# Products in two tiles, softmax four ahead and moved x loads: one change to a tuned convolution and two-layer product

## The chip, the cores and the metric

The kernel runs on one core of a Trainium2 chip. The time is the device time of one execution in microseconds (us). "Span" is the profiled execution from its first to its last instruction, about 1.8 us shorter than the time of the same run.

## The reference

```python
w = softmax(weight_gen, axis=-1)               # batch 8, 4096 tokens, 8 heads, 7 taps
x_pad = concat([zeros(6 tokens), x])           # 192 channels, 24 for each head
conv[s, h, g] = sum over k of w[s, h, k] * x_pad[s + k, h, g]
h = conv.reshape(32768, 192) @ w_in            # 192 x 2048
out = (h - tanh(h)) @ w_out                    # 2048 x 192, float32
```

## The kernel before

The 32768 tokens are cut into 32 superblocks of 1024. Each token's seven taps are multiplied by GpSimd. Some of the seven products are then added by DMAs that accumulate in SBUF ("first sum", "second sum"); TensorE transposes what is left and adds it up in PSUM ("the transposes"). Pass n of the loop runs the first product (line L354) of superblock n in 16 steps f, weaves in the second product (L389) of earlier blocks, and near its end, at steps 13 and 14, transposes superblock n+1 (L311). GpSimd meanwhile makes the products of n+2.

```python
xpool  = tile_pool(bufs=2)      # x
wgpool = tile_pool(bufs=2)      # weight_gen, its exponential e_t, the softmax wsm
ppool  = tile_pool(bufs=2)      # pr: one tile of all seven taps
TWO_SUMS = [n for n in range(13, NTOT) if n % 3]        # 13 superblocks
# ... products(n), from superblock 5 on:
mul(nc.gpsimd, 0, 2)
second_sum(n - 1)                       # taps 0,1 += taps 2,6   (n-1 in TWO_SUMS)
mul(nc.gpsimd, 2, 6)
dma_sum(pr, 0, 3, 3, 6)                 # first sum: taps 0-2 += taps 3-5
mul(nc.gpsimd, 6, K)
prods_of[n] = parts(0, 1) if n in TWO_SUMS else parts(6, 0, 1, 2)
# ... pass n:
f == 1:   softmax_exp(n + 3); load_wg(n + 4); products(n + 2)
f == 7:   load_x(n + 3, last_sub[0])    # from SyncE, behind the subtraction of step 7
f == 13:  transposes(n + 1, (0, 1))
f == 14:  transposes(n + 1, (2,))
```

The output of a superblock is stored once per pass, also from SyncE.

The softmax here doesn't subtract the row's maximum and nothing guards it: scores larger than these inputs give would overflow.

Of the kernel before, what the change touches and what calls it, by code (L numbers as in the profile page):

```python
# [16 lines left out]
def kernel(  # L17
# [18 lines left out]
    J = 8  # L36
# [6 lines left out]
    NC = D // R  # L43
    PLAIN = (0, 1)
    PART = tuple(range(2,5))
    TWO_SUMS = tuple([n for n in range(13,NTOT) if n%3])
    SUM_FIRST = tuple(range(5,32))
    SCALE_TWICE = True
# [4 lines left out]
    xpool = ctx.enter_context(tc.tile_pool(name="xpool", bufs=2))  # L53
    wgpool = ctx.enter_context(tc.tile_pool(name="wgpool", bufs=2))
    ppool = ctx.enter_context(tc.tile_pool(name="ppool", bufs=2))
    cpool = ctx.enter_context(tc.tile_pool(name="cpool", bufs=2))
# [28 lines left out]
    last_conv = {}  # L85
    first_halo = {}

    def order(inst, other, reason):
# [17 lines left out]
    def load_x(n, behind=None):  # L106
# [23 lines left out]
        if n == 0:  # L130
            rows(0, P, HALO, HALO + J)
            rows(16, P, 0, HALO)
            rows(1, 16, 0, HALO)
            no_halo()
        else:
            dma = rows(0, P)
            if behind is not None:
                order(dma, behind, "order of the loads")
            if s == 0:

                no_halo()
        x_of[n] = x_t

    def softmax_exp(n):
        wg_t = wg_of.pop(n)
        e_t = wgpool.tile([P, J, H, K], FP32, name="e_t")
        last_exp[0] = nc.scalar.activation(  # L147
            out=e_t[:].rearrange("p j h k -> p (j h k)"),
            in_=wg_t[:].rearrange("p j h k -> p (j h k)"),
            func=ACT.Exp,  # L150
        )
        e_of[n] = e_t

    def softmax_tile():
        return wgpool.tile([P, J, H, K], FP32, name="wsm")

# [14 lines left out]

    def softmax_norm(n, bank):

        wsm = softmax_tile()
        zr_v = bank[:, 512 - J * H : 512]
        nc.vector.reciprocal(zr_v, zsum_of[n][:])  # L176

        def finish():
            scale(nc.vector, wsm[:], e_of[n], zr_v)
            wsm_of[n] = (wsm, None, None, None)  # L180

        return finish

# [28 lines left out]

    def dma_sum(pr, k0, k1, src0, src1, step=1):
        nc.gpsimd.dma_start(  # L214
            out=pr[:, k0:k1].rearrange("p k j d -> p k (j d)"),
            in_=pr[:, src0:src1:step].rearrange("p k j d -> p k (j d)"),
            accum_op=mybir.AluOpType.add,
            max_dma_last_dim=2 * J * D,
        )

    def products(n, taps=None, sums=None, hooks={}):
# [5 lines left out]

        pr = ppool.tile([P, K, J, D], BF16, name="pr")
        x_v = x_t[:]
        step = x_v.ap[0]  # L230

        def mul(eng, k0, k1, j0=0, j1=J):

            w = wsm_v if eng is nc.vector else wsm[:]
            nj = j1 - j0
            return eng.tensor_mul(  # L236
                pr[:, k0:k1, j0:j1, :].rearrange("p k j (h g) -> p k (j h) g", h=H),
                bass.AP(
                    tensor=x_v.tensor,
                    offset=x_v.offset + (k0 + j0) * D,  # L240
                    ap=[step, [D, k1 - k0], [G, nj * H], [1, G]],
                ),
                w[:, j0:j1]
                .rearrange("p j h (k o) -> p k (j h) o", o=1)[:, k0:k1]
                .to_broadcast([P, k1 - k0, nj * H, G]),
            )

        def parts(*ks):
            return [[pr[:, k] for k in ks]] * NC

# [9 lines left out]

        if n in PLAIN:
            mul(nc.gpsimd, 0, 3)
            mul(nc.gpsimd, 3, 5)
            mul(nc.gpsimd, 5, K)
            prods_of[n] = parts(*range(K))
        elif n in PART:
            mul(nc.gpsimd, 0, 2)
            mul(nc.gpsimd, 2, 4)
            dma_sum(pr, 0, 2, 2, 4)
            mul(nc.gpsimd, 4, K)  # L270
            prods_of[n] = parts(4, 5, 6, 0, 1)
        else:
            mul(nc.gpsimd, 0, 2)
            second_sum(n - 1)
            mul(nc.gpsimd, 2, 6)
            if n in SUM_FIRST:
                dma_sum(pr, 0, 3, 3, 6)
            mul(nc.gpsimd, 6, K)
            if n not in SUM_FIRST:
                dma_sum(pr, 0, 3, 3, 6)  # L280
            if n in TWO_SUMS:
                to_sum[n] = pr
                prods_of[n] = parts(0, 1)
            else:
                prods_of[n] = parts(6, 0, 1, 2)
            if n == NTOT - 1:
                second_sum(n)

    def second_sum(n):

        if n in to_sum:
            dma_sum(to_sum.pop(n), 0, 2, 2, K, 4)

# [55 lines left out]
    def gemm1(n, f):  # L349
# [18 lines left out]
        last_sub[0] = nc.vector.tensor_sub(gt[:], ph_f, th[:])  # L368
        g_of.setdefault(n, []).append(gt)

    LAST = (NTOT - 1) * J
# [140 lines left out]
    for c in range(NC):  # L512
# [4 lines left out]
        1,  # L517
        taps=[(V, 0, 1, 0, J), (V, 1, 2, 0, J), (G_, 2, 5, 0, J), (G_, 5, 7, 0, J)],
        sums=range(K),
        hooks={2: load_w_out},  # L520
    )
# [3 lines left out]
    softmax_norm_ramp(2, obank[0])  # L525
    products(2)

# [30 lines left out]
    FIRST = dict(pairs=(4, 12, 0, 16, 1, 15, 0, 16, 0, 16, 0, 13, 3, 0, 16, 16), t1=(15, 2), t2=(11, 10), scale=15, sums=(1, 2, 3, 4, 8, 10))  # L558
    X_AT = 7

    def transposes(n, chunks):
# [4 lines left out]
        return pcs[0]  # L566

    for n in range(1, NTOT):
        more = n < NTOT - 1
        finish = None  # L570
        plan = FIRST if n == 1 else STEADY
        for f in range(NFT):
            gemm1(n, f)
            if n == 1:
# [8 lines left out]
                if f == 5:  # L583
                    wsm_of[3] = (softmax_tile(), None, e_of[3], zr_of[3])
                    products(3)
            elif f == 1:
                if n + 3 < NTOT:
                    softmax_exp(n + 3)
                if n + 4 < NTOT:
                    load_wg(n + 4)  # L590
                if n < NTOT - 2:
                    products(n + 2)
            if n > 1 and n + 3 < NTOT:
                for h, at in enumerate(plan["sums"]):
                    if f == at:
                        softmax_sum(n + 3, h * JH, (h + 1) * JH)
            if f == X_AT and n + 3 < NTOT:
                load_x(n + 3, last_sub[0])
            done = 0
            for chunks, at in sorted((((0, 1), plan["t2"]), ((2,), plan["t1"])), key=lambda c: c[1]):  # L600
                if more and at[0] == f:
                    out_pairs(at[1] - done)
                    done = at[1]
                    pc = transposes(n + 1, chunks)
                    if chunks == (2,) and n + 3 < NTOT:
                        finish = softmax_norm(n + 3, pc[:, 0])
            if finish is not None and f >= plan["scale"]:
                finish()
                finish = None
            out_pairs(plan["pairs"][f] - done)  # L610
# [36 lines left out]
```

## Time and profile before

| | before |
|---|---|
| median of the first 3 runs | 752.21 us (752.07 to 753.29) |
| span of the profiled run | 751.4 us, mean granted clock 0.994 |

Pass lengths and waits are read off in the prediction. Two more pieces of the same profile matter later. The first is part of the page's list of DMA issues (size of one, median time from issue to landing) with the row of the queue that brings instructions (packets, MB, share of the 16 engines' time):

```profile
q8 instruction: 109, 1.79, 0.9%
...
x_t<-in_x_dram SPq DMA_DIRECT2D x31, 1344.0 KB, 6.0
pr<-pr POOLq DMA_DIRECT2D x27, 1152.0 KB, 9.9
out_dram<-out_sb SPq DMA_DIRECT2D x31, 768.0 KB, 3.4
```

The second is who TensorE waited for between 60 and 747 us, beside the one wait for the second sum:

```profile
PE ph L354 <- issue: 0.6, 1, 0.6
PE obank L389 <- issue: 0.5, 2, 0.3
```

"issue" stands for time in which the engine waited for nothing that the profile knows.

### The profile page before, as it was taken

To read this page: it belongs to the slowest core of one execution; us is meant where nothing else is said; L and a number is where in the kernel's file an instruction comes from. 1 tells how busy PE (TensorE), PEld (TensorE's weight loads), DVE (VectorE), ACT (ScalarE), POOL (GpSimd) and SP (SyncE) were. 2 spreads that over 40 slices of the span, in tenths; PEclk is the share of its full clock that TensorE was granted. 3 is DMA by queue.
4 is the path that set the end of the run, shared out by engine and by line. 5 is a ranking of instruction groups with operands and counts; after the bars stand their busy time and mean duration, and the time that the engine had idled before them with its cause. 6 is when DMAs were issued, how large, how long until landed. Compare 5 with 4: busy or idle time off the path is not lost.

```text
span 751.4 us, 30497 instructions
## 1 busy us (share of the span) xinstructions
PE 725.4 (97%) x13928; PEld 567.6 (76%) x13928; DVE 664.6 (88%) x655; ACT 638.8 (85%) x872; POOL 668.9 (89%) x150
## 2 busy tenths in 40 slices
PE   3899999999999999999999999999999699999998
PEld 2477887787887777777777777777787577777777
DVE  7999889998889998999999999999989589998983
ACT  4888888888888888898989899898989588988883
POOL 7999999999999999999999999999999988999000
PEclk9999999999999999999999999999999899999999
DMA  8944526665655567785796777579668658673412
GB/s 234 242 111 107 171 109 173 187 181 126 191 149 170 169 170 160 202 196 163 196 229 151 180 203 185 169 196 215 173 157 192 180 139 189 183 177 85 113 44 86
DMA packets 32511, 124.99 MB, mean 166 GB/s; under 512 B 4495, under 2 KB 9343, under 8 KB 28414
## 3 DMA queue, kind: packets, MB, share of 16 engines
q0 software_dynamic: 17664, 46.01, 35.7%
q1 hardware_dynamic: 14718, 77.03, 27.6%
q8 instruction: 109, 1.79, 0.9%
q14 instruction: 20, 0.16, 0.1%
HBM read 54.52 MB, written 25.17 MB: 106 GB/s over the span
## 4 chain that ended last, share of the span: by engine, by line
PE 49%; DMA 4%; POOL 4%; issue 0%; ACT 0%; DVE 0%; POOLq 0%; DVEq 0%
PE obank L389 23%; PE ph L354 22%; DMA pr<-pr 4%; POOL pr L236 4%; PE pc L311 2%; PE po L432 1%; ACT th L367 0%; DVE wsm L207 0%; POOL pr L214 0%; ACT convT L337 0%; DVE pc L176 0%; DVE out_sb L446 0%; ACT ot L445 0%; DVE gt L368 0%; POOLq L214 0%
## 5 line engine op out<-in xcount | busy, mean ns | idle before, releaser
L368 DVE TENSOR_TENSOR gt<-ph,th 128x1024 bf16<-128x1024 f32 x512 | 603.1, 1218 | 66.8 <-ACT th L367 66.2
L236 POOL TENSOR_TENSOR pr<-x_t,wsm 128x3072 bf16<-128x3072 f32 (+3 forms) x95 | 629.7, 6816 | 8.1 <-PE obank L389 3.4
L367 ACT ACTIVATE th<-ph 128x1024 f32<-128x1024 f32 x512 | 506.8, 1026 | 71.1 <-PE ph L354 66.9
L354 PE MATMUL ph<-convT,w_in 64*128 64x512 bf16 x3072 | 407.3, 380 | 5.0 <-DVE gt L368 3.2
L389 PEld LDWEIGHTS <-gt 64*128 64x128 bf16 x7936 | 353.0, 94 | 73.0 <-issue 11.7
L389 PE MATMUL obank<-w_out,gt 64*128 64x192 bf16 x7936 | 399.5, 243 | 0.6 <-issue 0.5
L354 PEld LDWEIGHTS <-w_in 64*128 64x128 bf16 x3072 | 171.5, 95 | 82.7 <-issue 12.2
L408 ACT ACTIVATE out_sb<-obank 128x192 f32<-128x192 f32 x248 | 82.4, 332 | 12.9 <-PE obank L389 10.4
L214 POOL DMA_DIRECT2D pr<-pr x43 | 54.9, 1276 | 20.4 <-DMA pr<-pr 11.0
L311 PEld LDWEIGHTS <-pr 64*128 64x128 bf16 x2664 | 51.9, 102 | 24.1 <-POOL pr L236 10.2
L311 PE MATMUL pc<-ident,pr 64*128 64x64 bf16 x2496 | 50.7, 194 | 16.6 <-POOL pr L236 10.1
L337 ACT ACTIVATE convT<-pc 128x1024 bf16<-128x1024 f32 (+1 forms) x62 | 50.5, 816 | 7.3 <-PE pc L311 6.7
L161 DVE TENSOR_REDUCE zsum<-e_t 128x32 f32<-128x224 f32 (+1 forms) x61 | 23.6, 387 | 3.0 <-ACT e_t L147 3.0
L147 ACT ACTIVATE e_t<-wg_t 128x448 f32<-128x448 f32 x32 | 18.2, 569 | 7.3 <-DMA wg_t<-in_weight_gen_dram 7.3
L207 DVE TENSOR_TENSOR wsm<-e_t,pc 128x448 f32<-128x448 f32 x28 | 17.4, 621 | 3.3 <-POOL pr L236 0.5
L176 DVE RECIPROCAL pc<-zsum 128x64 f32<-128x64 f32 x28 | 15.4, 551 | 0.1
L432 PE MATMUL po<-w_out,gt 64*128 64x192 bf16 x256 | 11.2, 243 | 0.0
L236 DVE TENSOR_TENSOR pr<-x_t,obank 128x1536 bf16<-128x1536 f32 (+4 forms) x8 | 10.3, 1349 | 0.6 <-ACT wsm L199 0.6
L432 PEld LDWEIGHTS <-gt 64*128 64x128 bf16 x256 | 10.8, 93 | 0.0
L446 DVE TENSOR_TENSOR out_sb<-po,ot 128x192 f32<-128x192 f32 x8 | 2.9, 358 | 9.0 <-ACT ot L445 9.0
L445 ACT ACTIVATE ot<-po 128x192 f32<-128x192 f32 x8 | 2.6, 331 | 7.3 <-PE po L432 7.3
L467 POOL DMA_DIRECT2D w_in<-in_moe_w_in_dram x4 | 2.5, 628 | 3.0 <-ACT e_t L147 3.0
(19 smaller groups left out, 18.3 us busy)
## 6 DMA issues: line engine op xcount, KB each, us to landing
x_t<-in_x_dram SPq DMA_DIRECT2D x31, 1344.0 KB, 6.0
pr<-pr POOLq DMA_DIRECT2D x27, 1152.0 KB, 9.9
out_dram<-out_sb SPq DMA_DIRECT2D x31, 768.0 KB, 3.4
pr<-pr POOLq DMA_DIRECT2D x16, 768.0 KB, 6.8
wg_t<-in_weight_gen_dram SPq DMA_DIRECT2D x32, 224.0 KB, 6.8
x_t<-in_x_dram SPq DMA_DIRECT2D x1, 768.0 KB
w_out<-in_moe_w_out_dram POOLq DMA_DIRECT2D x1, 768.0 KB, 9.6
out_dram<-out_sb SPq DMA_DIRECT2D x4, 192.0 KB, 3.9
```

The costliest lines, as they stand in the source:

```text
L147: last_exp[0] = nc.scalar.activation(out=e_t[:].rearrange("p j h k -> p (j h k)"), in_=wg_t[:].rearrange("p j h k -> p (j h k)"), func=ACT ...
L161: nc.vector.reduce_sum(out=zsum_of[n][:, j0 * H : j1 * H], in_=e_of[n][:, j0:j1].rearrange("p j h k -> p (j h) k"), axis=AX.X,)
L214: nc.gpsimd.dma_start(out=pr[:, k0:k1].rearrange("p k j d -> p k (j d)"), in_=pr[:, src0:src1:step].rearrange("p k j d -> p k (j d)"), acc ...
L236: return eng.tensor_mul(pr[:, k0:k1, j0:j1, :].rearrange("p k j (h g) -> p k (j h) g", h=H), bass.AP(tensor=x_v.tensor, offset=x_v.offset ...
L311: nc.tensor.matmul(pc[r][:, col : col + R] if home else pc[:, r, col : col + R], lhsT=prods[c][gi][r * R : (r + 1) * R, 2 * j : 2 * j + 2] ...
L337: last_conv[0] = nc.scalar.activation(out=out, in_=pc[:, :, 0:cols].rearrange("p r (cj t) -> p r cj t", t=R), func=ACT.Copy,)
L354: nc.tensor.matmul(ph[:, r, :], lhsT=w_in[r * R : (r + 1) * R, c, f * P : (f + 1) * P], rhs=convT[r * R : (r + 1) * R, c, :], start=(c == ...
L367: last_act[0] = nc.scalar.activation(out=th[:], in_=ph_f, func=ACT.Tanh)
L368: last_sub[0] = nc.vector.tensor_sub(gt[:], ph_f, th[:])
L389: mm = nc.tensor.matmul(po[:, 0:D], lhsT=g_of[n][f][r * R : (r + 1) * R, col : col + P], rhs=w_out[r * R : (r + 1) * R, f, :], start=(r == ...
L408: last_act[0] = nc.scalar.activation(out=out_sb[:, j, :], in_=po[:, 0:D], func=ACT.Copy)
L432: nc.tensor.matmul(po[:, r, 0:D], lhsT=g_of[n][f][r * R : (r + 1) * R, col : col + P], rhs=w_out[r * R : (r + 1) * R, f, :], start=(f == 0 ...
```

## The change

Its intent: GpSimd loses ground to TensorE from superblock 16 on (66.3 to 67.1 us for three superblocks, against 65.86) and cannot save up a lead (being ahead of TensorE) before, because softmax weights come only three passes ahead and seven-tap tiles are held twice. So the seven taps go to two tiles (four taps three times, three taps once), the softmax runs four ahead with four buffers, the multiplications are cut 2, 2, 3, second sums start at 16, and the x load moves so that it lies between the first sum and the second. The core of the diff (cuts marked):

```diff
-    TWO_SUMS = tuple([n for n in range(13,NTOT) if n%3])
+    TWO_SUMS = (16, 17, 19, 20, 22, 23, 25, 26, 28, 29, 31)
+    AHEAD = 4
-    wgpool = ctx.enter_context(tc.tile_pool(name="wgpool", bufs=2))
-    ppool = ctx.enter_context(tc.tile_pool(name="ppool", bufs=2))
+    wgpool = ctx.enter_context(tc.tile_pool(name="wgpool", bufs=3))
+    papool = ctx.enter_context(tc.tile_pool(name="papool", bufs=3))
+    pbpool = ctx.enter_context(tc.tile_pool(name="pbpool", bufs=1))
+    wspool = ctx.enter_context(tc.tile_pool(name="wspool", bufs=4))
 ... (exponential in place in wg_t; products of superblocks 0 and 1 rearranged)
-            mul(nc.gpsimd, 0, 2)
-            second_sum(n - 1)
-            mul(nc.gpsimd, 2, 6)
-            dma_sum(pr, 0, 3, 3, 6)
-            mul(nc.gpsimd, 6, K)
+        x_after[n + 1] = mul(nc.gpsimd, 0, KH)      # KH = 2
+        mul(nc.gpsimd, KH, KA)                      # KA = 4
+        second_sum(n - 1)
+            mul(nc.gpsimd, KA, K)
+            dma_sum(pa[:, 0:3], pb[:, 0:3])
 ... (pass n)
-            if f == X_AT and n + 3 < NTOT:          # X_AT = 7
-                load_x(n + 3, last_sub[0])
+            if f == (9 if n == 1 else 1):
+                emit_x(n + 3)                       # behind the first multiplication of n + 2
+                if soft and n != AHEAD and soft[0] + 1 < NTOT and n > 1:
+                    load_wg(soft[0] + 1)
```

## The prediction

> **What bounds the kernel now.** I read the busy totals first, then the row of 40 slices, then who waited for whom, then one window per superblock, and last the chain of waits around the one window that stands out.

> ```profile
> PE 725.4 (97%) x13928; PEld 567.6 (76%) x13928; DVE 664.6 (88%) x655; ACT 638.8 (85%) x872; POOL 668.9 (89%) x150
> PE   3899999999999999999999999999999699999998
> ```

> TensorE is at nine tenths or more in nearly every slice; only one slice late in the run (slice 31, 582 to 601 us) drops to 6. A busy TensorE need not be at its peak, so I checked rates in the chain: twelve 64x512 matmuls of the first product take 1.29 to 1.30 us (six pairs on two row tiles, 215 ns a pair), 32 of 64x192 of the second take 1.32 us, 64 small transposes 0.93 us. These repeat unchanged. So TensorE sets the pace, and only its gaps and its work can change.

> A superblock is 1024 tokens; there are 32 (0 to 31). Loop pass n runs the matmuls of superblock n and near its end the transposes of n+1. I cut the time at the output stores, which SyncE issues once per pass; the columns of the windows are the stretch, its length, and busy time by engine.

> ```profile
> 268.28:290.68 22.40, 22.40 (x452) 17.62 (x449) 20.36 (x21) 19.82 (x28) 20.87 (x5) 1.00 0.59 162
> 290.68:313.69 23.01, 22.26 (x404) 17.51 (x401) 20.36 (x21) 19.75 (x28) 21.77 (x6) 1.00 0.75 188
> 313.69:335.42 21.73, 21.73 (x404) 16.56 (x402) 20.34 (x21) 19.60 (x28) 21.43 (x6) 1.00 0.75 190
> ...
> 532.98:555.67 22.69, 22.62 (x452) 17.97 (x449) 20.36 (x21) 19.98 (x28) 22.39 (x6) 1.00 0.65 172
> 555.67:577.40 21.73, 21.73 (x404) 17.61 (x401) 20.29 (x21) 19.60 (x28) 20.14 (x5) 1.00 0.74 187
> 577.40:607.98 30.58, 24.61 (x404) 18.85 (x401) 20.53 (x21) 20.13 (x28) 26.67 (x7) 0.89 0.79 175
> ```

> Two lengths are to be seen: 22.40 us where the superblock prepared has four tap groups to transpose (452 matmuls) and 21.73 us where a second sum by DMA leaves two (404). The difference of 48 matmuls is worth 0.67 us. Superblocks 13 to 31 not divisible by three have the second sum, 13 of them. One pass, which prepares superblock 26, takes 30.58 us in place of 21.73, and one, for 13, takes 23.01. Why, the waits of 577 to 608 us and the chain say:

> ```profile
> PE pc L311 <- DMA pr<-pr: 6.0, 1, 6.0
> POOL pr L214 <- DMA pr<-pr: 1.6, 1, 1.6
> ```

> ```profile
> 574.19 10.84 DMA pr<-pr
> 585.03 0.02 issue
> 585.05 0.02 POOLq L214
> 585.07 0.49 issue
> 585.56 11.34 DMA pr<-pr
> 596.90 0.14 issue
> 597.04 1.04 PE pc L311 x32
> ```

> The products come from GpSimd. The first sum of 26 was out at 574.19 and landed after 10.84 us; GpSimd waited for it 1.6 us before it could issue the second sum at 585.56. An x load was issued at 586.00, the second sum took 11.34 us against a median of 6.8, and TensorE stood 6.0 us. The remaining 2.9 us of the 8.85 are the restart: the pipeline behind the transposes refills, with a mean clock of 0.89 in the window. Since superblock 16 GpSimd has fallen behind: from 16 to 19, 19 to 22 and 22 to 25 its products start 66.3, 66.6 and 67.1 us apart, while three passes of TensorE are 21.73+21.73+22.40 = 65.86 us. The stand is this debt coming due.

> [...] a second sum takes 6.5 us alone, 11.3 beside an x load. [...]

> **The change part by part.** (1) Fewer second sums: they start at 16, so 13 and 14 go from two groups to four: 2 x 0.67 = +1.34 us of TensorE time, certain.

> (2) GpSimd work. Its multiplications of 2, 4 and 1 taps become 2, 2 and 3, the same elements: 5.6+5.6+8.7 = 19.9 us (before's superblocks 2 to 4 already run these sizes), and a DMA issue adds some 1.1 us with its wait. So 21.05 us with one sum and 21.8 with two, if no DMA makes it wait. Three superblocks: 21.05+2x21.8 = 64.7 against TensorE's 65.86. GpSimd would gain 1.2 us on TensorE per three, where before it lost up to 1.2.

> (3) The second sum of n now goes out after two multiplications of n+1 (11.2 us), not one (5.6). From issue of the first sum to that of the second: 12 us, against 3.4+0.3+5.6+0.5, about 10, before. First sums take 8.8 to 11.5, so the GpSimd waits (11.0 us in total, 6.2 of them at the very end) vanish. The price: the second sum leaves later, so more lead is needed.

> (4) The lead. Softmax four ahead, with four wsm buffers, makes the weights of n one pass earlier; three buffers of four taps in place of two of seven let GpSimd run a superblock further. Before, GpSimd stood at superblocks 13, 14 and 15 for weights (1.23, 1.23 and 0.94 us), so it could not save what it gained. The 1.28 us lost in the window from 290.68 is the other side: VectorE's weight scaling waits for GpSimd to release a wsm buffer (0.5 us), and TensorE behind it. With four buffers this goes: -1.28.

> (5) The x load of n+1 waits for the first multiplication of n, so it starts 5.7 us after a superblock's start and lies mostly between the first sum (out at -0.8) and the second (out at +11.2). A second sum beside a whole x load, as at 585.56, no longer occurs: with (2) to (4) that is -8.85 us, and -0.29 for the pass before it but one.

> Does the lead suffice? Before, superblock 4's last product ends at 95.1 us. The reordered start (three GpSimd instructions for superblock 1 in place of two) adds about 0.75, so superblock 5 starts at 95.9 and, at 21.05 each, 16 at 327.5. Its second sum goes out at 327.5+21.05+11.2 = 359.8 and lands at 366 to 370. TensorE wants it 8.5 us before its store, at about 370.6. It just fits, and afterwards the margin grows.

> (6) New costs, small. Superblock 5 now has its first sum after its last multiplication, out at about 116.1; with 10 us it lands at 126, wanted at 124.9: about +1.2. Pass 4 makes two softmaxes: VectorE 20.36 + 0.76+0.55+0.62 = 22.29 of 22.40 us, estimate +0.3. In pass 2 the weight_gen load queues on SyncE behind an x load that waits for GpSimd: out at 80.8, 7 us, wanted at 87.5: up to +0.5.

> Sum: -8.85-1.28-0.29+1.34+1.2+0.3+0.5 = -7.1. From 752.2: **745.1 us**, 0.9% faster.

> **The rivals.** (a) The single buffer of three taps becomes the bound: GpSimd must not write it until the previous first sum has landed. It has 11.3 us, or 12.1 with a second sum; sums take 8.8 alone and 10.5 to 11.5 with a neighbour. If x load and output store both meet it, say 12.5 us, GpSimd loses a microsecond per superblock, its surplus of 1.35 shrinks, and from 16 on TensorE waits again: 748 to 753. I give this one in six. (b) The later second sum comes too late in general: the 366 to 370 against 370.6 above leaves almost nothing. A miss costs once, since TensorE's slip gives GpSimd the lead: 1 to 4 us, 746 to 749. (c) The SyncE queue: an x load held for GpSimd holds weights and the output store behind it. Stores have some 10 us of slack, weights 2 to 4; a few stalls of 1 us, 746 to 748. (d) Nothing but gaps counts and all new costs vanish: -9.1, 743.1. More than that has no source: the start (TensorE's first real gap, 9.3 us) and the tail are hardly touched.

> **Range and chances.** Reaching 737.5 (2%) needs 14.7 us, and the gaps named sum to 10.4 before the +1.34; only a gain in the ramp could do it. Being 2% slower needs GpSimd to lose 0.6 us or more per superblock throughout, beyond the debt of today. So 742.0 to 750.0 eight times in ten; faster 0.03, within 2% 0.95, slower 0.02.

> **What would show it right or wrong.** Right: no pass over 23.5 us between 112 us and the end; passes of 22.40 up to superblock 15 and 21.73/21.73/22.40 after; 2760 transposes (96 more); no TensorE wait for a sum over 2 us; second sums near 7 to 8 us; GpSimd at 64.7 us per three superblocks. Wrong: GpSimd's second or third multiplication idle behind a sum (rival a); TensorE waiting for the sum at 5 or at 16 by several us (b); ScalarE's exponential waiting for weight_gen (c); or VectorE binding pass 4.

## The result, and the profile after

| | before | after |
|---|---|---|
| median (lowest to highest, runs) | 752.75 us (752.07 to 755.36, 4) | 761.82 us (758.92 to 765.24, 4) |
| span and clock of the profiled run | 751.4 us, 0.994 | 763.5 us, 0.995 |

The ratio is 1.0116 with a 95% interval of 1.0066 to 1.0165: slower by 1.2%, inside the 2% band, but outside the range of 742 to 750. All ratios here are the mean time of one kernel's fast runs over that of the other's in the same rounds, so they are not quite the ratios of the medians quoted beside them. The profiled run of the changed kernel, 765.24 us, is the slowest of its four.

GpSimd's order of work came out as predicted. The list of GpSimd's work around superblock 16 (start, duration, what, and the wait before it in brackets) shows the multiplications, the first sum and the second sum:

```profile
329.61 11.69 POOL L253 TENSOR_TENSOR pa<-x_t,wsm 128x3072 bf16<-128x3072 f32 x2
340.78 8.82 POOL L253 TENSOR_TENSOR pb<-x_t,wsm 128x4608 bf16<-128x4608 f32 x1
349.89 1.29 POOL L219 DMA_DIRECT2D pa<-pb  x1 [0.30 <-DVE wsm L212]
350.71 11.71 POOL L253 TENSOR_TENSOR pa<-x_t,wsm 128x3072 bf16<-128x3072 f32 x2
361.86 1.72 POOL L219 DMA_DIRECT2D pa<-pa  x1
362.64 9.32 POOL L253 TENSOR_TENSOR pb<-x_t,wsm 128x4608 bf16<-128x4608 f32 x1
...
373.07 6.12 POOL L253 TENSOR_TENSOR pa<-x_t,wsm 128x3072 bf16<-128x3072 f32 x1
```

Superblock 16 starts at 329.61 (predicted 327.5), the next 21.1 us later, and no multiplication waits for a sum. Superblock 17, which issues a second sum, takes 22.4 us (350.71 to 373.07), not the 21.8 of the prediction; what follows from that is said in the part on why the prediction was wrong. The stand of before is gone. And yet TensorE has more holes, not fewer. Its totals and its row of 40 slices:

```profile
PE 729.1 (96%) x14024; PEld 576.4 (75%) x14024; DVE 665.6 (87%) x655; ACT 639.5 (84%) x872; POOL 665.7 (87%) x149
...
PE   3899899989999999999999999999999999999997
...
q8 instruction: 109, 1.79, 1.0%
```

Slices that read 8 instead of 9 are new. The matmul count is up by 96, as predicted. The waits of TensorE between 85 and 512 us (line, what it waited for: total, times, longest):

```profile
PE obank L415 <- issue: 11.2, 7, 2.4
...
PE obank L415 <- ACT out_sb L434: 2.0, 1, 2.0
PE pc L336 <- issue: 1.7, 2, 1.5
```

No sum is in the list. The big entry is "issue", which was 1.1 us in all of before. The windows of single passes, cut where ScalarE begins the second copy of a pass's transposes (convT, L362; stretch, length, busy time by engine, granted clock, DMA share, GB/s), say where:

```profile
82.36:109.20 26.84, 23.31 (x476) 17.96 (x474) 21.34 (x21) 20.02 (x28) 24.01 (x6) 1.00 0.63 187
109.20:131.84 22.64, 22.64 (x451) 17.23 (x449) 19.89 (x22) 20.31 (x28) 22.34 (x5) 1.00 0.62 146
131.84:159.14 27.30, 23.42 (x450) 18.81 (x448) 22.69 (x23) 20.27 (x28) 27.00 (x5) 0.98 0.66 161
159.14:182.90 23.76, 23.76 (x451) 19.71 (x449) 19.41 (x20) 19.84 (x28) 23.16 (x7) 0.95 0.63 154
182.90:205.30 22.40, 22.40 (x451) 17.63 (x449) 20.36 (x21) 19.82 (x29) 22.10 (x5) 1.00 0.71 173
272.56:298.84 26.28, 22.84 (x451) 18.71 (x449) 21.52 (x21) 20.05 (x29) 25.98 (x6) 1.00 0.70 202
298.84:321.24 22.40, 22.40 (x451) 18.75 (x449) 19.31 (x20) 19.81 (x27) 22.10 (x6) 1.00 0.66 158
321.24:347.50 26.26, 24.33 (x452) 20.09 (x450) 20.49 (x21) 20.04 (x29) 25.96 (x5) 0.94 0.57 148
480.40:504.40 24.00, 22.30 (x448) 17.40 (x446) 21.44 (x21) 19.94 (x28) 23.41 (x7) 1.00 0.85 184
```

Most passes have the predicted 22.40 or 21.73 us, so TensorE's steady rate is as predicted. Four windows take 26 to 27 us and two some 24. Counted from first product to first product, passes 3 to 20 (84.11 to 506.16 us) take 422.05 us against 400.9 at the usual lengths, 21.2 us too much. The first long window has a reason that I had named. SyncE's issues:

```profile
79.93 0.36 SPq L119 DMA_DIRECT2D x_t<-in_x_dram  x1
80.41 1.42 SPq L105 DMA_DIRECT2D wg_t<-in_weight_gen_dram  x1
81.88 1.44 SPq L438 DMA_DIRECT2D out_dram<-out_sb  x1
```

The weight_gen load goes out right behind the x load and beside the store, lands 8.8 us later, and ScalarE's exponential waits 2.35 us for it; TensorE stops for as long (87.82 to 90.17). The others look like this, in TensorE's list from 131.5 us:

```profile
131.62 0.84 PE L379 MATMUL ph<-convT,w_in 64*128 64x512 bf16 x6
132.27 1.15 PE L415 MATMUL obank<-w_out,gt 64*128 64x192 bf16 x23
134.93 0.57 PE L415 MATMUL obank<-w_out,gt 64*128 64x192 bf16 x9 [1.51 <-issue]
```

A run of 32 second-product matmuls is broken after the 23rd, in the middle of one block's accumulation. All operands have been there for long; nothing in the program distinguishes the 24th from the 23rd.

### What the "issue" stops are

I numbered TensorE's records in the trace from 0 by their start (28,048 weight loads and matmuls and 17 of its sequencer) and looked at the number at which each stop of over 0.6 us ends; a stop is counted from the start of one record to the start of the next. (This and the other tables in plain fences are counted from the trace, not lines of the profile.)

```
changed kernel         stop at (us)       length   number   number mod 256
                       106.71 - 108.43     1.72      3521       193
                       133.17 - 134.93     1.76      4545       193
                       155.40 - 158.01     2.61      5313       193
                       273.90 - 275.95     2.05      9921       193
                       296.14 - 298.01     1.88     10689       193
                       322.57 - 324.75     2.17     11713       193
                       501.61 - 503.54     1.94     18369       193     sum 14.13
weights (named above)   87.82 -  90.17     2.35      2835        19
kernel before          290.80 - 291.81     1.01     10945       193
```

The trace also gives the deadline. No packet starts before TensorE has passed about number 170 of a block (168 at the earliest), and one that is late stops TensorE at number 193 of the next. So I take it that the fetch is asked at about 170, and that it has the time of 279 instructions: the lead. It is 7.5 us in the median before and 8.0 after (stops inside a lead counted), and only 4.1 to 5.5 us for the few blocks that hold most of a pass's transposes, which are short instructions (64 take 0.93 us, where 32 matmuls of the second product take 1.32). The page counts the packets of GpSimd's queue (q0, 33.7% in the changed kernel), of SyncE's (q1, 30.4%) and of the fetch (q8, 1.0%) as shares of the same 16 DMA engines. How late the packet starts after being asked goes with what these engines are doing. By what was under way, and how much of it was still to come:

```
                                       before             after
under way when asked               blocks  late us    blocks  late us
nothing                               28     1.08        28     0.97
SyncE queue, under 4 us to come       37     1.57         7     2.57
SyncE queue, 4 us or more              0       -         18     3.97
a sum, under 4 us to come             17     2.89        14     2.68
a sum, 4 us or more                   13     4.30        22     3.97
```

(Blocks with both under way are left out. Counted again with another rule for when a transfer is under way, the rows move by up to four blocks and 0.3 us, so a few tenths between rows mean nothing; what stays is about 1 us with nothing under way and about 4 with much still to come.) The packet itself and the time from its end to TensorE's restart are together 2.2 to 2.5 us at the seven stops, so a block with a lead of 4.58 us can afford to be some 2.3 us late. Take the stop at 133.17: asked at 128.6, 3.84 late, 0.87 for the packet, 1.62 after it, is 6.33; minus 4.58 is the 1.75 us measured. All seven stops are at blocks whose lead is 5.4 us or less. In the changed kernel 16 blocks between 60 and 740 us have such a lead (under 5.5 us), and 11 of them were asked while a transfer was under way, sums and loads alike. In before 15 have it; twelve met traffic of the SyncE queue, all with under 4 us to come, and none was asked while a sum was under way. A short lead is not needed if the packet is late enough: before's own stop of 1.01 us is at a lead of 6.8 us, with the packet 5.5 us late. The load and the store of the changed kernel also take longer from issue to landing than before:

```profile
x_t<-in_x_dram SPq DMA_DIRECT2D x24, 1344.0 KB, 8.3
...
out_dram<-out_sb SPq DMA_DIRECT2D x31, 768.0 KB, 9.0
```

The store, 3.4 us before, takes 9.0 us now. In 23 of the 30 passes whose store is issued between 60 and 740 us it goes out within 4.1 us of an x load; before, it was 6.3 us or more from any. The packets start 3.6 to 5.6 us after being asked at the seven stops; why it is that long no run here shows.

The account: the predicted gains and the 1.34 us for 96 transposes came in size (-8.85, -1.28, -0.29, +1.34, together -9.1). The losses are 21.2: 2.35 for weights, 14.1 for seven fetch stops, and by subtraction 4.7, which I put down to the restarts (two of the windows with or just after a stop show a granted clock of 0.95 and 0.94). -9.1 + 21.2 is +12.1; the spans differ by 12.1. Terms of under 1 us on both sides are left out, so the match to a tenth is chance.

### The profile page after: what moved, and what is told of

Read it like the earlier page. It is cut to its first block, busy times and chain, and to the rows that moved or that the text cites.

```text
span 763.5 us, 30693 instructions
## 1 busy us (share of the span) xinstructions
PE 729.1 (96%) x14024; PEld 576.4 (75%) x14024; DVE 665.6 (87%) x655; ACT 639.5 (84%) x872; POOL 665.7 (87%) x149
## 3 DMA queue, kind: packets, MB, share of 16 engines
q0 software_dynamic: 17120, 44.44, 33.7%
q1 hardware_dynamic: 15040, 77.00, 30.4%
## 4 chain that ended last, share of the span: by engine, by line
PE 92%; DVE 3%; DMA 2%; issue 2%; ACT 1%; ACTq 0%; DVEq 0%
PE obank L415 43%; PE ph L379 42%; PE pc L336 5%; DMA wg_t<-in_weight_gen_dram 2%; PE po L458 1%; DVE gt L393 1%; DMA x_t<-in_x_dram 1%; ACT th L392 0%; DVE pb L253 0%; DVE pa L253 0%; DVE wsm L212 0%; DVE zsum L166 0%; DVE obank L194 0%; ACT convT L354 0%; ACT wg_t L152 0%
## 5 line engine op out<-in xcount | busy, mean ns | idle before, releaser
L415 PE MATMUL obank<-w_out,gt 64*128 64x192 bf16 x7936 | 402.8, 243 | 13.4 <-issue 11.2
L253 POOL TENSOR_TENSOR pa<-x_t,wsm 128x3072 bf16<-128x3072 f32 (+1 forms) x63 | 358.1, 5875 | 2.5 <-PE obank L415 2.3
L253 POOL TENSOR_TENSOR pb<-x_t,wsm 128x4608 bf16<-128x4608 f32 (+2 forms) x33 | 277.4, 8406 | 3.0 <-PE pc L336 2.5
L434 ACT ACTIVATE out_sb<-obank 128x192 f32<-128x192 f32 x248 | 82.3, 332 | 25.8 <-PE obank L415 23.3
L362 ACT ACTIVATE convT<-pc 128x1024 bf16<-128x1024 f32 (+1 forms) x62 | 50.5, 816 | 3.7 <-PE pc L336 3.1
L336 PEld LDWEIGHTS <-pa 64*128 64x128 bf16 x2400 | 46.4, 101 | 8.7 <-issue 1.1
L336 PE MATMUL pc<-ident,pa 64*128 64x64 bf16 x2304 | 46.9, 193 | 1.8 <-POOL pa L253 0.8
L219 POOL DMA_DIRECT2D pa<-pb x27 | 34.7, 1287 | 8.8 <-POOL pb L253 7.3
L219 POOL DMA_DIRECT2D pa<-pa x14 | 19.6, 1402 | 11.0 <-DMA pa<-pb 10.1
L166 DVE TENSOR_REDUCE zsum<-wg_t 128x32 f32<-128x224 f32 (+1 forms) x61 | 23.6, 388 | 3.0 <-ACT wg_t L152 3.0
L152 ACT ACTIVATE wg_t<-wg_t 128x448 f32<-128x448 f32 x32 | 18.2, 569 | 9.6 <-DMA wg_t<-in_weight_gen_dram 9.6
L212 DVE TENSOR_TENSOR wsm<-wg_t,pc 128x448 f32<-128x448 f32 x28 | 17.3, 621 | 2.8
L336 PEld LDWEIGHTS <-pb 64*128 64x128 bf16 x360 | 7.7, 105 | 11.7 <-POOL pb L253 9.3
L458 PE MATMUL po<-w_out,gt 64*128 64x192 bf16 x256 | 11.2, 243 | 0.0
## 6 DMA issues: line engine op xcount, KB each, us to landing
pa<-pb POOLq DMA_DIRECT2D x27, 1152.0 KB, 10.4
```

Of the source, the lines that this page charges most:

```text
L152: last_exp[0] = nc.scalar.activation(out=wg_t[:].rearrange("p j h k -> p (j h k)"), in_=wg_t[:].rearrange("p j h k -> p (j h k)"), func=AC ...
L166: nc.vector.reduce_sum(out=zsum_of[n][:, j0 * H : j1 * H], in_=e_of[n][:, j0:j1].rearrange("p j h k -> p (j h) k"), axis=AX.X,)
L219: return nc.gpsimd.dma_start(out=out.rearrange("p k j d -> p k (j d)"), in_=in_.rearrange("p k j d -> p k (j d)"), accum_op=mybir.AluOpTyp ...
L253: return eng.tensor_mul(prod(k0, k1)[:, :, j0:j1].rearrange("p k j (h g) -> p k (j h) g", h=H), bass.AP(tensor=x_v.tensor, offset=x_v.offs ...
L336: nc.tensor.matmul(pc[r][:, col : col + R] if home else pc[:, r, col : col + R], lhsT=prods[c][gi][r * R : (r + 1) * R, 2 * j : 2 * j + 2] ...
L362: last_conv[0] = nc.scalar.activation(out=out, in_=pc[:, :, 0:cols].rearrange("p r (cj t) -> p r cj t", t=R), func=ACT.Copy,)
```

## The experiments

There were 18 runs, one of them the changed kernel again, all in comparison with the kernel before on the same chip. The theories, in words: the stops come from late instruction blocks (rival: from waits that the profile cannot name, such as the weights or the SyncE order); they are late because of the x loads, whose place now drifts with GpSimd (rivals: because of the sums; because of a burst of several transfers; because of the mere alignment of the blocks with the program). The texts name theories by letter as they stood at that batch.

### First batch: the place of the x load

**x back to step 7.** The changed kernel, x behind the subtraction of step 7.

```diff
+            if f == 7 and n + 3 < NTOT:
+                load_x(n + 3, last_sub[0])
             if f == (9 if n == 1 else 1):
-                emit_x(n + 3)
```

> The changed kernel, but the x loads tied to TensorE again (f tile 7 of the pass, behind the subtraction), weight_gen loads left at f tile 1 and so no longer behind x. Theory A (TensorE starves for instructions: its 256-instruction blocks come through the same DMA engines, and x loads that follow GpSimd sit next to the first sum and before the transposes, where a block is used up fastest): at most two gaps of over 1 us in TensorE without a named releaser between 60 us and the end, no wait for weight_gen in pass 3, 743 to 748 us. Theory B (the later sums and their new tiles starve the fetches, x loads are innocent): five or more such gaps stay, 755 to 762 us. Theory C (only the SyncE order, weights behind x): the gaps stay but the 2.35 us wait goes, 757 to 760 us.

Measured: 774.98 us (772.65 to 779.37, 4 runs), ratio 1.0297, slower. Its waits over the whole run:

```profile
POOL pa L253 <- DMA x_t<-in_x_dram: 17.6, 9, 5.6
...
PE pc L336 <- DMA pa<-pa: 9.1, 3, 6.1
PE obank L415 <- issue: 8.9, 8, 2.6
```

The stops for late blocks stay, and new waits come: x at a place fixed to TensorE arrives too late for a GpSimd that runs ahead. The theory that the load's place alone does it (743 to 748 us) missed. Putting the load back is no cure.

**Weights ahead of x.** The two issues on SyncE change places.

```diff
             if f == (9 if n == 1 else 1):
-                emit_x(n + 3)
                 if soft and n != AHEAD and soft[0] + 1 < NTOT and n > 1:
                     load_wg(soft[0] + 1)
+                emit_x(n + 3)
```

> The changed kernel with two lines swapped: weight_gen is issued ahead of the x load at f tile 1. Theories A and B: only the wait of 2.35 us in pass 3 and its restart go, about 4 us: 755 to 760 us, with the gaps without a releaser still there (four to eight). Theory C (the SyncE order is the whole loss): 743 to 748 us and no gaps.

Measured: 758.39 us (757.80 to 759.22, 4), ratio 1.0071 (1.0027 to 1.0114). The wait for weights is gone (in pass 3 TensorE now stops 1.1 us behind the output store); from 85 to 512 us the "issue" waits stay:

```profile
PE obank L415 <- issue: 8.7, 6, 2.6
```

Five fetch stops of over 1 us are left, at 130, 152, 313, 336 and 493 us, all at number 193. So the order on SyncE is worth about 3 us, as the medians have it, and is not the main cause.

**The kernel before with the late x load.** x behind GpSimd's first multiplication.

```diff
-            mul(nc.gpsimd, 0, 2)
+            x_after[n + 1] = mul(nc.gpsimd, 0, 2)
 ...
-            if f == X_AT and n + 3 < NTOT:
-                load_x(n + 3, last_sub[0])
+            if f == (X_AT if n == 1 else 1) and n + 3 < NTOT:
+                load_x(n + 3, x_after.pop(n + 3))
```

> The kernel before with only its x loads tied to GpSimd (behind the first multiplication of the superblock before, issued at f tile 1), weights still ahead of x. Theory A: gaps without a releaser appear, three or more of 1 to 2.5 us, and the time rises to 757 to 770 us, unless the stand at superblock 26 goes (then 750 to 758 with the gaps). Theory B or C: no more than the one gap of before, 743 to 753 us.

Measured: 795.80 us (792.01 to 796.73, 6), ratio 1.057, slower. A miss as a test of the stops: only three or four are there, and the time goes to something else.

```profile
PE pc L312 <- DMA pr<-pr: 28.3, 10, 4.0
...
pr<-pr POOLq DMA_DIRECT2D x16, 768.0 KB, 13.5
```

The second sums take 13.5 us in the median, 6.8 before, and TensorE waits for them ten times. That it is the moved load which slows them, and that the change bears this place only by its lead, is my reading; the run does not separate the two.

**Thin x.** The changed kernel, x loads of 2 of the 14 token rows from superblock 6 on (a wrong result; the old tiles are read).

```diff
-            dma = rows(16 if s == 0 else 0, P)
+            dma = rows(16 if s == 0 else 0, P, 0, 2 if n > 5 else HALO + J)
```

> The changed kernel with x loads of a seventh of the bytes from superblock 6 on (two of fourteen rows, into the two tiles loaded before; a wrong result on purpose), order and waits kept. Theory A: traffic is what delays the fetches, so the gaps fall to two or fewer and the time to 745 to 751 us (the wait for weights in pass 3 may stay, it precedes most thin loads). If the wait or the order and not the traffic of the x loads did it: gaps stay, 757 to 764 us. Theory B: gaps stay.

Measured: 754.83 us (754.66 to 754.97, 4), ratio 1.0022 (0.998 to 1.0065). Fetch stops of over 0.6 us sum to 8.3 us, against 14.1 in the first profile of the changed kernel but 9.3 in its repeat below. So the x loads are not the whole cause, and one profile doesn't size their share.

### Second batch: quiet engines, other alignment, other order

**No sums and thin x.** Weights first, thin x, and from superblock 6 no sums (wrong; the number of TensorE's matmuls is unchanged).

```diff
-                dma_sum(pa[:, 0:3], pb[:, 0:3])
+                if n < 6:
+                    dma_sum(pa[:, 0:3], pb[:, 0:3])
 ... (second_sum issues nothing, x as in the experiment before)
```

> The changed kernel with weights ahead of x, thin x loads and from superblock 6 on no sums by DMA at all (TensorE still transposes the same groups; a wrong result on purpose). Theory A, now wider (every gap is a 256-instruction block of TensorE that is fetched late because sums or loads occupy the DMA engines when the block's lead, the time TensorE takes from asking to needing it, is short): no gap of 0.6 us or more without a releaser after superblock 6, passes of 22.40 and 21.73 us, 742 to 746 us, so the predicted gain is there once the fetches are in time. If the fetches are late for another reason (their own spacing, TensorE's pattern): gaps stay, 750 us or more.

Measured: 745.26 us (745.10 to 745.89, 4), ratio 0.9898 (0.9882 to 0.9915). TensorE's totals and slices:

```profile
PE 722.3 (97%) x14024; PEld 560.6 (75%) x14024; DVE 664.5 (89%) x655; ACT 638.6 (86%) x872; POOL 617.5 (83%) x112
...
PE   3799999999999999999999999999999999999997
```

No stop of over 0.6 us is left between 135 us and the last microseconds, and blocks start 0.9 us late on average between 60 and 740 us (2.8 in the changed kernel, 2.0 in before). This is the decisive run: the same weight loads and matmuls in almost the same instruction blocks (eleven of TensorE's semaphore records are missing, the first after 388 us), and with quiet DMA engines the stops are gone. What is left of TensorE's waits from 85 to 512 us:

```profile
PE obank L420 <- ACT out_sb L439: 0.7, 1, 0.7
PE ph L384 <- DVE wsm L216: 0.6, 1, 0.6
```

That it takes 745.26 us, and that I had predicted 745.1, is in part luck. This run has no sums after superblock 5, so it can't show that they would have been in time.

**128 more TensorE instructions at the start.** Weights first, and 64 matmuls on the identity ahead of everything, each with its weight load.

```diff
+    for i in range(64):
+        nc.tensor.matmul(obank[1][:, 0:R], lhsT=ident[0:R, :], rhs=ident[0:R, 0:R], start=True, stop=True)
```

> The kernel with weights ahead of x, and 64 matmuls without effect at the very start, in time TensorE is idle: this shifts every block boundary by 128 instructions against the passes. Theory A: gaps again start at instruction 193 of a block of 256, and so at other places of the program: the two largest of the kernel without the shift (2.05 us at 130 and 2.84 us at 313 us) are gone, others appear in other passes; the time may go either way, 750 to 765 us. If the gaps belong to places in the program or to what the DMA queues do then, and not to block boundaries: they stay near 130 and 313 us.

Measured: 762.08 us (759.71 to 766.43, 4), ratio 1.0127. Every instruction of the program has moved by half a block. The stops of over 0.6 us are still at 193 modulo 256, all eleven of them, so at other places of the program (108, 249, 271 and 320 us among them). It is the block boundary that stops TensorE, not the instruction that happens to stand there.

**x behind weights and store.** x at step 2.

```diff
+            if f == (9 if n == 1 else 2):
+                emit_x(n + 3)                      # no longer at f == 1
```

> The changed kernel with SyncE's order weights, output store, then x (x issued from f tile 2), so that the store no longer waits for GpSimd and joins the x load in one burst. Theory A: shorter bursts, fewer late fetches: 749 to 758 us, and no wait for weights. If only sums matter for the gaps: as with weights first alone, 757 to 760 us.

Measured: 762.44 us (759.09 to 766.92, 4), ratio 1.0129. The idea that it is the burst of three transfers from SyncE fell: with x behind the store there are eight fetch stops of over 0.6 us, and TensorE also waits 1.4 us for late sums.

**The last third of the transposes a step later**, to lengthen the lead of the blocks that hold them.

```diff
-    STEADY = dict(..., t1=(14, 8), t2=(13, 0), scale=14, sums=(2, 5))
+    STEADY = dict(..., t1=(15, 0), t2=(13, 0), scale=15, sums=(2, 5))
```

> The kernel with weights ahead of x, and the last third of the transposes moved from f tile 14 to the start of f tile 15, so that a block that spans a pass's end is used up more slowly (lead 4.6 us before, an estimate of 5.4 after, from the durations of the matmuls that come between). Theory A: the gaps of 1.5 us and more become rare, in total 3 to 6 us less gap: 750 to 757 us, unless the later eviction makes TensorE wait at the pass's start (then 758 or more, with a wait for convT). If the lead has no part in it: 757 to 760 us.

Measured: 756.62 us (756.28 to 760.31, 4), ratio 1.0064 against 1.0071 of the kernel it is built on. The shortest leads stayed at 4.5 to 4.6 us, so my estimate of the effect was wrong and the run tells nothing for or against.

### Third batch: leads, and three x buffers

**Transposes in three places.** For four-group superblocks from 6 on, at steps 10, 12 and 14.

```diff
+                (((0,), (10, 0)), ((1,), (12, 0)), ((2,), (14, 8)))     # these
-                (((0, 1), plan["t2"]), ((2,), plan["t1"]))              # before
```

> The kernel with weights ahead of x, and in passes from 6 on that prepare a four-group superblock the transposes in three equal parts at f tiles 10, 12 and 14 instead of two thirds and one third at 13 and 14. The lead of a block at a pass's end grows from 4.6 us to some 6.5 us (estimate from the matmul durations), above lateness (about 3.5 us under a sum or load) plus the 2.4 us from the packet's start to use. Theory A: no gap over 1.2 us in passes 6 to 14, those at 130 and 153 us stay, 752 to 756 us. If lead has no part: gaps as with weights first alone, 757 to 760 us.

Measured: 765.47 us (764.79 to 769.60, 4), ratio 1.0199, unclear. In passes 6 to 14, where it applies, only two stops of about 1 us are left, as the lead explains. But the change costs more than it saves (waits from 85 to 512 us):

```profile
PE pc L336 <- DVE gt L393: 6.4, 11, 0.6
```

With a third transposes tile in PSUM TensorE stops until VectorE frees a slot (the 6.4 us in 11 waits above), and these passes take 23.3 us in place of 22.4.

**The kernel before, with the 128 instructions at its start.** The same edit as above.

> The kernel before with the 64 matmuls without effect at the start, which shift its block boundaries by 128 instructions. Theory A says the kernel before was spared because its nine short-lead blocks (4.1 to 4.6 us) happened to be asked for when the DMA engines were quiet (mean lateness 1.2 us): with the shift other passes get the short leads; two or more gaps at instruction 193 of a block and 753 to 762 us if they meet sums; as before, 751 to 755 us, if they do not. Rival: the kernel before is safe by its structure (fixed place of the x loads): at most one gap, 751 to 754 us.

Measured: 753.94 us (751.82 to 764.8, 20, one of them slow), ratio 1.0026 (1.0006 to 1.0045). Two stops of 0.79 and 0.68 us, and TensorE's wait for a second sum now at 459 us. So in two alignments the kernel before is spared, which one alignment's luck does not explain.

**x at step 7 with three x buffers**, once with spread transposes and once without.

```diff
-    xpool = ctx.enter_context(tc.tile_pool(name="xpool", bufs=2))
+    xpool = ctx.enter_context(tc.tile_pool(name="xpool", bufs=3))
```

> Three x buffers, x loads at f tile 7, weights at f tile 1, and the spread transposes. Theory A: x traffic away from the pass's end and long leads: few gaps, 745 to 752 us, which would beat both kernels. If sums and x loads collide (second sums of 10 us or more, or the single three-tap buffer holding GpSimd): 753 to 765 us.

> The kernel with x loads at f tile 7 (which took 775 us), with three x buffers instead of two. If its loss came from GpSimd waiting for x (17.6 us in its trace) because two buffers and a fixed place hold the lead back: those waits go and so do most waits of TensorE for sums, 752 to 762 us with the late fetches left. If the x loads at f tile 7 slow the sums themselves: waits for sums of 5 us or more stay, 765 us or more.

Measured: 778.52 us (774.01 to 783.05, 4), ratio 1.0361, and 777.28 us (772.96 to 779.86, 4), ratio 1.033, both slower. GpSimd still waits 28 to 32 us for x in each. It was the issue at step 7 of pass n for superblock n+3 that came too late, not the lack of a buffer.

### Fourth batch: what is left when x is punctual

**x four ahead at step 7, three buffers.** In the changed kernel.

```diff
+            if f == (9 if n == 1 else 7) and n + 4 < NTOT:
+                load_x(n + 4, last_sub[0])        # in place of emit_x(n + 3)
```

> The changed kernel with three x buffers and the x load of n+4 (not n+3) at f tile 7 of pass n, weights at f tile 1. GpSimd keeps its lead and never waits for x, and the x loads stay in mid-pass. If the drifting x loads are the main cause of the late fetches: one to three gaps of a microsecond or more at block boundaries, all under a sum, 744 to 752 us. If the sums alone do it once GpSimd leads: five or more gaps, 754 to 762 us. If x loads in mid-pass collide with the second sums: waits for sums, 755 us or more.

Measured: 769.86 us (766.62 to 773.55, 4), ratio 1.0235 (1.0181 to 1.0289), unclear. Here x has before's place in the pass, GpSimd never waits for it, no steady sum is late, and the stops are worse than in any other profile. The time fits only the third of my forecasts, and its sign, waits for sums, is absent. TensorE's waits over the whole run:

```profile
PE obank L415 <- issue: 16.1, 11, 3.0
```

Of its 16 blocks with a lead under 5.5 us nine were stopped, for 18.2 us. So the drifting place of x is not the cause: that form of the theory fell.

**No sums, full x.** Weights first, no sums from superblock 6 (wrong).

> Weights ahead of x, full x loads behind GpSimd, no sums by DMA from superblock 6 on (a wrong result on purpose). If late fetches need sums: as the run with neither, 745 to 747 us. If x loads alone suffice (load-only lateness 3.6 us in the changed kernel): two to five gaps stay, 748 to 754 us.

Measured: 748.18 us (746.29 to 749.20, 12), ratio 0.9952 (0.9929 to 0.9975). One stop of this kind is left, early, at 129.5 us:

```profile
PE obank L416 <- issue: 2.3, 1, 2.3
```

Set side by side:

| | full x | thin x |
|---|---|---|
| sums | 758.4 | 754.8 (weights behind x) |
| no sums from 6 | 748.2 | 745.3 |

Taking the sums away is worth 9 to 10 us, thinning x 3 to 4. The four ran on three chips, on which the kernel before took 752.3 to 753.3 us. The table can't be read as a clean split. Without sums GpSimd runs ahead until it waits for VectorE and TensorE (24 us from 85 to 512 us), which should tie its phase, and with it the place of the x loads, to the pass.

**The changed kernel once more**, as it is.

> The changed kernel unaltered, for a comparison on one chip and its own spread: 758 to 766 us, six to eight gaps at block boundaries and the wait for weights in pass 3 in any profile; the boundaries hit may differ from the first profile, as they depend on when transfers meet fetches.

Measured: 760.95 us (755.99 to 763.76, 4), ratio 1.0127. The profiled run, 755.99 us, has four fetch stops at 193 (1.59, 2.59, 2.98 and 2.11 us, sum 9.3) and a weights stop of 0.80. The first profile, 765.24 us, had 14.1 and 2.35. The two profiles differ by 9.25 us, of which these stops are 6.4; restarts would be the natural rest, which was not traced. So between these two profiles the stops are most of the difference.

### Fifth batch: the kernel before with fewer second sums, and a third alignment

**Second sums from 16, and second sums in every other superblock.**

```diff
-    TWO_SUMS = tuple([n for n in range(13,NTOT) if n%3])          # 13 superblocks
+    TWO_SUMS = tuple([n for n in range(16,NTOT) if n%3])          # the first of the two: 11
+    TWO_SUMS = tuple([n for n in range(13,NTOT) if n%2==0])       # the second: 9
```

> The kernel before with one part of the change alone: second sums from superblock 16, so 11 instead of 13. +1.34 us of TensorE for certain. If GpSimd's debt per three superblocks (0.4 to 1.2 us) is only begun three superblocks later: the stand comes later or meets no x load and goes, 744 to 753 us, gaps at block boundaries as before (none to two). If the stand comes all the same: 752 to 755 us.

> The kernel before with a second sum in every other superblock from 14 (9 instead of 13): +2.68 us of TensorE (4 x 0.67). GpSimd then needs about 21.1 + 22.3 = 43.4 us for two superblocks against TensorE's 44.13, so it runs up no debt and no stand is left: -8.85 us and less of the VectorE wait at 310 us: 745 to 748 us, which would beat both kernels without a deeper lead. If the stand comes from the x load meeting a second sum whatever the debt: 751 us or more.

Measured: from 16, 754.55 us (745.92 to 758.55, 16 runs, one slow), ratio 1.001 (0.9978 to 1.0043). The stand is still there, 7.2 us at 528 us, and so is one fetch stop of 0.98 us. In every other superblock, **747.44 us (745.55 to 749.40, 20), ratio 0.9939 (0.9917 to 0.996)**, against 752.82 us of the kernel before on that chip. TensorE's waits between 60 and 740 us and its slices:

```profile
PE ph L354 <- issue: 0.7, 1, 0.7
PE obank L389 <- issue: 0.5, 2, 0.3
```

```profile
PE   3899999999999999999999999999999999999998
```

No stand, and one fetch stop of 1.06 us at 291 us (the first line), as in before. Four superblocks more with four groups cost 4 x 0.67 = 2.7 us of transposes, and the stand of 8.85 us goes: -6.2 worked out, -5.4 measured between the medians. One changed line on the kernel before beats both kernels in the median, by 0.6% over the kernel before, inside the 2% band.

One thing about the kernel before must be added. In the last three batches its own runs come in two groups: 16 of 72 take 745.5 to 749.8 us, the others 751 or more (here 8 of 34). No profile of the lower group was kept, so what it lacks, the stand perhaps, is not shown. The changed line brings 20 of 20 runs under 750 us, where before has about one in five there.

**64 more instructions** (32 matmuls) on the changed kernel with weights first.

> The changed kernel with weights ahead of x and 32 matmuls without effect at the start: boundaries shifted by 64 instructions. If the loss depends on which passes get the short leads, the number of gaps over 1.2 us changes between three and eight and the time lies in 750 to 765 us; gaps start at instruction 193 of a block again.

Measured: 763.93 us (760.94 to 766.11, 4), ratio 1.0189, unclear. Again all its ten stops of over 0.6 us are at 193 modulo 256. Three alignments of the changed program give 758 to 764 us; two of before give 753 to 754.

## Why the prediction was wrong

**What bounds the kernel: right, but one limit was missing.** TensorE sets the pace, at the 22.40 and 21.73 us per pass that were read off; the changed kernel keeps them wherever it isn't stopped. "Only its gaps and its work can change" was right too. But gaps were sought only where an operand is late. A late instruction is a gap as well.

**Part 1 (+1.34) and part 3: right.** There are 96 more transposes, and no multiplication waits for a sum (one wait of 10.1 us, for the last sum of all, stays at the end).

**Part 2, GpSimd's rate: wrong from superblock 16 on.** A superblock with one sum takes 21.1 us, as worked out. But three superblocks with two second sums take 65.8 to 67.8 us, not 64.7 (the three-tap multiplication behind a second sum alone takes 9.3 us, not 8.8), so GpSimd goes on losing to TensorE's 65.86 and gains nothing. "Afterwards the margin grows" is not seen either. The second sums land 15 to 20 us before TensorE uses them, because the stops had held TensorE back by some 16 us when superblock 16 was transposed (388.06 us, 372.09 in the quiet run). Set against the quiet run's transposes, the same landings would be 1.6 us early at 16 and 1.0, 3.2 and 0.4 us late at 22, 26 and 29. That is an estimate from two traces; but that the lead suffices without the stops was not shown.

**Part 4, the lead: GpSimd's waits for weights are gone, but the 1.28 us were misread.** In before's window from 290.68 the profile has

```profile
291.81 0.37 PE L354 MATMUL ph<-convT,w_in 64*128 64x512 bf16 x1 [0.64 <-issue]
```

This is before's fetch stop at number 10945. The step in which it lies takes 2.10 us (from 289.72), where the same step one pass on takes 1.29 (from 312.74). So the stop is 0.81 us of the 1.28. The weight scaling that I had named accounts for about 0.3. So the limit that broke the prediction was in the profile it was made from, under another name. The pass for superblock 13 does take 22.40 us in the changed kernel.

**Part 5, the x load, right in what it removes (the 8.85 us, with the doubt of part 2), and the step that failed in what it adds.** The prediction moved x and sums by GpSimd's clock and asked only whether data would come in time for the next consumer. It had no term for what these transfers do to the third user of the same DMA engines, the fetch of TensorE's instructions. Measured: seven stops of 1.7 to 2.6 us, 14.1 us together, and some 4.7 us of restart. With the sums and most of x taken away the stops are gone and the time is 745.26 us.

**Part 6: the weights were the right wait and too small.** "Up to +0.5" measured 2.35 in the first profile and 0.80 in the second, because the load took 8.8 us, not 7, beside an x load and a store. The +1.2 for superblock 5 did not come: TensorE was late itself by then, and the sum landed at 127.90 us, just as the transposes began. The +0.3 for pass 4 can be seen in the quiet run, as the 0.6 us for which TensorE waits for VectorE's second weight scaling.

**The rivals.** (a) did not occur, (c) did. (b) did not occur either, but TensorE's lateness hid whether it would have. (d), at 743.1, is not reached even by the quiet run. None had the fetch. The "wrong" signs listed at the end of the prediction would have shown only (c); the sign "no pass over 23.5 us" was the one that failed.

**What is shown and what is not.** Shown: the stops are late 16 KB blocks of instructions (the 193 modulo 256 in three alignments and many kernels); the seven of the first profile are at leads of 5.4 us or less with a transfer still running, and with sums and most of x gone, the stops go. Other profiles have stops at longer leads too, up to 9.5 us with a packet 8.2 us late (x back to step 7). Not shown: how the blame is shared between sums and loads (taking the sums away leaves one stop, but shifts the x loads too); and why before's sums did not fall on the short blocks. I take it that its GpSimd, held to TensorE by the three-ahead weights and two product tiles, issues its sums at a favourable time of the pass, and that the new lead lets them drift; that is argued. No run cut the lead of the changed kernel back to three passes, which would test it. Nor is it shown how the DMA engines queue the fetch, so that it starts 4 to 8 us late.

## What to carry to other kernels

Where an engine issues as many short instructions as TensorE does here (28,048), count the fetch as one more user of the DMA engines: work out the shortest time in which the engine goes through a lead of instructions (here, of 279, 4.1 us), and see what transfers can be running then (here the packets started about 1 us late with nothing under way, and about 4 us late with 4 us or more to come). When a profile shows a wait for nothing in the middle of a uniform run of instructions, number the instructions and look at the remainder modulo 256 (here 193 at all seven stops) before looking for a data wait. And before rearranging a pipeline to pay off a debt of a few microseconds, try doing a little less of what makes the debt: here one line, nine second sums in place of thirteen, gave 5.4 us between the medians, of the 7.1 that the change was meant to give.
